# Attention and two feed-forward layers on one core: a planner that counts TensorE's turns between kinds of work

## Chip, core and metric

The kernel runs on one core of a Trainium2 chip. The metric is the device time of one execution in microseconds (us); lower is better.

## What is computed

Decayed causal attention (4 batches, 8 heads, 576 positions, head size 64), then two feed-forward layers over the 2304 tokens, all float32. Cut to what matters:

```python
scores = q @ k.T / sqrt(64) + cum[:, None] - cum[None, :]   # cum = cumsum(log f); causal
x = softmax(scores) @ v                       # heads side by side: (2304, 512)
h = x @ w_in                                  # (2304, 1024)
solu = h * softmax(h)
ln = (solu - mean) / sqrt(var + 1e-6) * g_ln
x2 = ln @ w_out                               # (2304, 512)
out = maximum(x2 @ w2_in, 0) ** 2 @ w2_out    # inner size 2048
```

## The kernel before

**Tiles.** Queries are cut into 20 tiles, five a batch: four of 128 rows and one of 64 (last in batches 0 and 2, first in 1 and 3). Tile n has eight heads; "n2h4" below is head 4 of tile 2.

**Steps on TensorE.** For each head `head` adds a step `scores` (L505: two matmuls, four where there are over 512 keys, float32r) and a step `flip` (L560: one transpose per block of keys, of the exponentials). For each pair of heads `mix` adds the product with the values (L581: plain float32, two TensorE records for each matmul), and after a tile's last pair `spread` (L608: four transposes). For each finished 128 tokens `first` adds the products with `w_in` (L808 to L810, 24 matmuls: "in" below), two steps of transposes (L885), and by way of `out1` the products with `w_out` (L749 to L751). `step` adds the second layer (up: L1146 to L1148, down: L1176 to L1178).

**Between them** VectorE takes a row minimum (L523, L526), ScalarE the exponential (L540) and most copies out of PSUM (L314). ScalarE, VectorE and GpSimd also turn Q, K and the weights into pairs of float32r (L316, L434, L661 to L679). `scores` writes PSUM banks z0 and z1; all transposes and `out1` share three banks (pp); the transposed exponentials go to a ring of three tiles (pt), so the copy for head s waits until the `mix` that read head s-3 is done.

**What sets the order.** No engine's order is written by hand. Each step is recorded by `Plan.add` with a duration on each engine, a due time `prio` and what it reads and writes; `Plan.lay` then places all of them, always the action that can start first. On each engine it takes the earliest start t0 of all candidates and, of those within `slack` (20 ns) of it, the one with the smallest `prio`:

```python
t0 = min(c[0] for c in cand)
c = min((c for c in cand if c[0] <= t0 + slack), key=lambda c: (c[1].prio, c[1].no))
```

For TensorE the end of a step follows from `pe_end`, which models a clock that halves after little work. Each engine then runs its instructions in that order. In the plan before, a step's duration depends on the step alone; `mix` carries a flat 200 ns.

Of the kernel before, what the change touches and what calls it, by code (L numbers as in the profile page):

```python
# [21 lines left out]


class Step:
    __slots__ = ("eng", "fn", "prio", "deps", "succ", "left", "rdy", "start", "end", "take", "uses", "on", "no", "late", "weak", "port")


class Plan:
# [10 lines left out]
        pe=dict(pe=0, dve=196, act=215, pool=200, dma=1100),  # L39
# [5 lines left out]

    TICK, DUTY = 10240 / 3, 1280.0

    def __init__(self, slots, banks):
        self.banks = banks
        self.steps = []  # L50
        self.writer = {}
        self.readers = {}
        self.slots = slots
        self.users = {}
        self.slot = {}

    def add(self, eng, fn, prio, reads=(), writes=(), take=None, uses=(), late=0, port=False):

        s = Step()
        s.eng, s.fn, s.prio, s.take, s.no, s.late = eng, fn, prio, take, len(self.steps), late
        deps = {}
        s.uses = tuple(uses) + ((take,) if take else ())
        for k in s.uses:
            self.users.setdefault(k, []).append(s)
        s.weak, s.port = None, port
        for k in reads:
            if k in self.writer:
                deps[self.writer[k].no] = self.writer[k]  # L70
            rs = self.readers.setdefault(k, [])
            if k in self.banks or k[0] == "pp":

                if rs and rs[-1].no not in deps:
                    s.weak = rs[-1]
                    deps[s.weak.no] = s.weak
            rs.append(s)
        for k in writes:
            if k in self.writer:
                deps[self.writer[k].no] = self.writer[k]  # L80
            for r in self.readers.get(k, ()):
                deps[r.no] = r
        for k in writes:
            self.writer[k] = s
            self.readers[k] = []
        deps.pop(s.no, None)
        s.deps = list(deps.values())
        s.succ = []
        for d in s.deps:
            d.succ.append(s)  # L90
        s.left = len(s.deps)
        s.rdy = {}
        s.end = None
        self.steps.append(s)
        return s

    def lay(self, slack=60):
# [48 lines left out]
                ready(s)  # L146
        todo = len(self.steps)
        port = 0.0
        order = []
        while todo:  # L150
            pick = None
            for e in engs:
                cand = []
                for s in avail[e]:
                    t = max(free[e], s.rdy[e])
# [15 lines left out]
                    cand.append((t, s, i))  # L171
                if not cand:
                    continue
                t0 = min(c[0] for c in cand)
                c = min((c for c in cand if c[0] <= t0 + slack), key=lambda c: (c[1].prio, c[1].no))
                if e != "pe":

                    end = c[0] + c[1].eng[e]
# [8 lines left out]
                if e == "pool":  # L187
# [5 lines left out]
                    ]  # L193
                    if any(y < end and end - y > (y - c[0]) * WORTH for y in x):
                        continue
                done = pe_end(c[0], c[1].eng[e], False) if e == "pe" else c[0] + c[1].eng[e]
                if pick is None or (c[0], done) < (pick[0], pick[4]):
                    pick = (c[0], c[1], c[2], e, done)
            assert pick, "the plan is stuck"
            t, s, i, e, done = pick  # L200
            if e == "pe":
                pe_end(t, s.eng[e], True)
            s.on, s.start, s.end = e, t, done
            free[e] = done
            if e == "dve" and s.port and s.eng[e]:
# [17 lines left out]
def tile_kernel(ctx: ExitStack, tc: tile.TileContext, q, k, v, f, w_in, w_out, g_ln, w2_in, w2_out, out):  # L223
# [257 lines left out]
    def head(s):  # L481
# [27 lines left out]
            rk += kcells(c, j, k0, k0 + ext)  # L509
        for c, k_ in zip(cuts, zk):  # L510
            mm = 0.4375 * rep * (c[2] - c[1]) + 6
            pl.add(dict(pe=2 * mm), lambda c=c: scores(c), prio, rk, [k_])
        st = ST[s % NST]
        su = SU[n % 2]
        adj = ADJ[s % NADJ]
# [37 lines left out]
        for g in range(0, nb, per):  # L553
            e = min(nb, g + per)
            sk = key()

            def flip(g=g, e=e, sk=sk):
                for c in range(g, e):
                    zc = zcol(T, c)
                    nc.tensor.transpose(at(sk)[:, (c - g) * m : (c - g + 1) * m], adj[0:m, zc : zc + P], ident[0:m, 0:m])  # L560

            pl.add(dict(pe=(e - g) * 109 * m / P), flip, prio - 200, ak + ["adjz"], [sk], take=sk)
            w = (e - g) * m
            copy(
                w, lambda g=g, e=e: pt[:, g * m : e * m], lambda sk=sk, w=w: at(sk)[:, 0:w], prio - 200, [sk],
                [("pt", s % NPT, g)], [sk],
            )


    def mix(s):  # L570
# [14 lines left out]
                    )  # L585

        rk = [("pt", (s - i) % NPT, g) for i in (0, 1) for g in range(5)] + [("vn", vslot[b, c]) for c in range(t + 1)]
        pl.add(dict(pe=(t + 1) * 218 * m / P + 200), fn, prio, rk, ["xo"])
        if p == NP - 1:
            i = T["x"] % XB  # L590
            w = slice(off, off + m)
# [32 lines left out]
                DM, lambda: X[0:m].rearrange("p c (j d) -> p (c j) d", d=D),  # L624
                lambda: su[0:m, 2].unsqueeze(2).broadcast_to([m, H, D]), prio - 300, [uk], ["x"], psum=False,
            )
            pl.add(dict(pe=NP * 109 * m / P), spread, prio - 300, ["x", "ident"], [sk], take=sk)
            copy(
                NP * m, lambda: X[:, :, 0:m], lambda: at(sk).rearrange("p (c x) -> p c x", x=P)[:, :, 0:m], prio - 300,
                [sk], ["x"], [sk],  # L630
# [162 lines left out]
    def first(x):  # L793
# [82 lines left out]
        for g in range(KF // 4):  # L876
# [15 lines left out]


            extra = [("lnr", y, z) for y in range(4) for z in "lh"] + [("lnw", y) for y in range(4)] if x == 0 else []
            pl.add(dict(pe=436), flips, t2 + g * 50, ["e", "ident"], [ck] + extra, take=ck)
            copy(
                512, lambda g=g: LN["h"][:, 4 * g : 4 * g + 4, x % 3, :],
                lambda ck=ck: at(ck).rearrange("p (c x) -> p c x", x=P), t2 + g * 50, [ck], [("lnh", x % 3, g)], [ck],
# [485 lines left out]

DUE, WORTH = 400, 1.0

_INS = ["q", "k", "v", "f", "moe_w_in", "moe_w_out", "moe_g_ln", "moe2_w_in", "moe2_w_out"]
_OUTS = [((2304, 512), "float32")]
# [43 lines left out]
```

## Time and profile before

| | |
|---|---|
| median of 3 runs | 875.02 us (873.55 to 877.12) |
| profiled execution | 874.1 us, its span 872.0 us |
| TensorE busy | 838.4 us (96%) |
| weight loads / VectorE / ScalarE / GpSimd busy | 83% / 52% / 56% / 33% |
| granted TensorE clock, mean | 0.987 |

The span runs from the first instruction to the last; the execution's time is 2.1 us more. A matmul's own duration overlaps that of the next one, so what a matmul costs TensorE is read from one start to the next.

### The profile page before, as it was taken

The page shows a single profiled execution, that of the slowest core. Times are in us where ns is not written, and L with a number is a line of the kernel's source. Part 1 is how long each engine was busy: PE and PEld are TensorE (multiplying, and loading weights), DVE is VectorE, ACT ScalarE, POOL GpSimd, SP SyncE. Part 2 cuts the span into 40 slices and gives each one's busy share as a digit, 9 for nine tenths or more (in the row PEclk, how much of TensorE's full clock was granted, in tenths as well). Part 3 has the DMA queues.
Part 4 walks back from the last instruction along what each step waited for, and adds up shares of the span by engine and source line. Part 5 has one row for each costly group of instructions (what it writes and reads, how often), then busy time and mean ns, then how long its engine had stood idle before and what let it go on. Part 6 is the DMA issues. An engine that isn't in the chain of part 4 may idle for free.

```text
span 872.0 us, 15164 instructions
## 1 busy us (share of the span) xinstructions
PE 838.4 (96%) x5360; PEld 727.3 (83%) x5360; DVE 449.1 (52%) x1152; ACT 485.1 (56%) x1237; POOL 283.5 (33%) x375
## 2 busy tenths in 40 slices
PE   4878999999999999999999999999999999999998
PEld 2556877888888887888898988989999999999997
DVE  7888776766766666865657475122222222222221
ACT  6899887777877667777656474224223223223222
POOL 7577765534643345433346474000000000000000
PEclk9998997999999999999999999999999999999999
DMA  6633343333542236332475630015003002000001
GB/s 210 197 96 104 112 138 112 122 103 99 168 140 86 86 92 181 109 105 89 137 224 175 194 116 6 1 35 183 1 1 109 0 2 97 13 1 12 26 0 37
DMA packets 61260, 81.04 MB, mean 93 GB/s; under 512 B 8096, under 2 KB 40352, under 8 KB 61184
## 3 DMA queue, kind: packets, MB, share of 16 engines
q1 hardware_dynamic: 61184, 80.07, 29.8%
q8 instruction: 42, 0.69, 0.3%
q14 instruction: 34, 0.28, 0.1%
HBM read 60.44 MB, written 19.55 MB: 92 GB/s over the span
## 4 chain that ended last, share of the span: by engine, by line
PE 85%; ACT 6%; DVE 4%; issue 2%; POOL 2%; DMA 1%; ACTq 0%; POOLq 0%; DVEq 0%
PE pp L1148 7%; PE pp L1147 7%; PE pp L1146 7%; PE pp L560 6%; PE xo L581 6%; PE z L505 6%; PE pp L749 4%; PE hp L808 4%; PE pp L750 3%; PE pp L751 3%; PE hp L810 3%; PE hp L809 3%; PE z L1176 2%; PE z L1178 2%; PE z L1177 2%
## 5 line engine op out<-in xcount | busy, mean ns | idle before, releaser
L1154 ACT ACTIVATE q<-pp 128x384 f32<-128x384 f32 x96 | 47.1, 490 | 242.4 <-PE pp L1148 240.0
L1157 DVE CAST q<-q 128x384 fp32r<-128x384 f32 x96 | 38.7, 403 | 267.5 <-PE xo L1178 92.3
L540 ACT ACTIVATE adj<-z,st 64x288 f32<-64x288 f32 (+9 forms) x192 | 95.0, 497 | 28.9 <-DVE st L526 27.6
L505 PE MATMUL z<-k,q 128*128 128x256 f32 (+17 forms) x384 | 96.4, 350 | 8.2 <-DVE q L470 8.2
L560 PE MATMUL pp<-ident,adj 128*128 128x128 f32 (+1 forms) x480 | 80.5, 284 | 15.5 <-ACT adj L540 14.6
L314 ACT COPY pt<-pp 128x256 f32<-128x256 f32 (+5 forms) x170 | 68.8, 422 | 35.6 <-PE pp L560 33.2
L560 PEld LDWEIGHTS pp<-ident,adj 128*128 128x128 f32 (+1 forms) x480 | 54.7, 146 | 36.3 <-ACT adj L540 24.3
L749 PE MATMUL pp<-ln,woh 128*128 128x256 f32 x288 | 83.4, 290 | 0.0
L526 DVE CUSTOM_DVE_ANT_0 z<-z,maskb 128x128 f32<-128x128 f32 (+8 forms) x144 | 65.8, 463 | 34.3 <-PE z L505 31.9
L750 PE MATMUL pp<-ln,wol 128*128 128x256 f32 x288 | 80.2, 279 | 0.0
L751 PE MATMUL pp<-ln,woh 128*128 128x256 f32 x288 | 80.2, 278 | 0.0
L505 PEld LDWEIGHTS z<-k,q 128*128 128x128 f32 (+3 forms) x384 | 59.8, 192 | 15.6 <-ACT pt L1267 8.2
L581 PE MATMUL xo<-pt,vn 128*64 128x128 f32 (+1 forms) x960 | 70.0, 279 | 0.2 <-ACT pt L314 0.2
L581 PEld LDWEIGHTS xo<-pt,vn 128*64 128x64 f32 x960 | 50.5, 141 | 19.9 <-issue 13.7
L808 PE MATMUL hp<-wih,xl 128*128 128x512 f32 x144 | 61.7, 428 | 1.8 <-ACT hp L847 1.0
L809 PE MATMUL hp<-wil,xh 128*128 128x512 f32 x144 | 57.6, 400 | 0.9 <-POOL wil L679 0.9
L810 PE MATMUL hp<-wih,xh 128*128 128x512 f32 x144 | 57.5, 399 | 0.0
L749 PEld LDWEIGHTS pp<-ln,woh 128*128 128x128 f32 x288 | 54.3, 188 | 2.7 <-issue 1.5
L750 PEld LDWEIGHTS pp<-ln,wol 128*128 128x128 f32 x288 | 54.3, 189 | 0.4
L751 PEld LDWEIGHTS pp<-ln,woh 128*128 128x128 f32 x288 | 54.2, 188 | 0.0
L1156 ACT ACTIVATE q<-q 128x384 f32<-128x384 f32 x96 | 50.4, 525 | 2.9
L540 ACT ACTIVATION_READ_ACCUMULATOR adj<-z,st 128x1 f32 (+1 forms) x192 | 37.8, 197 | 0.0
(503 smaller groups left out, 2180.2 us busy)
## 6 DMA issues: line engine op xcount, KB each, us to landing
x2d<-xc SPq DMA_DIRECT2D x72, 128.0 KB
kn<-in_k_dram SPq DMA_DIRECT2D x32, 256.0 KB
ws<-in_moe_w_out_dram SPq DMA_DIRECT2D x28, 256.0 KB
vn<-in_v_dram SPq DMA_DIRECT2D x20, 256.0 KB
ws<-in_moe_w_in_dram SPq DMA_DIRECT2D x20, 256.0 KB
ln<-x2d SPq DMA_DIRECT2D x24, 192.0 KB
out_dram<-pt SPq DMA_DIRECT2D x18, 256.0 KB
qn<-in_q_dram SPq DMA_DIRECT2D x16, 256.0 KB
```

Of the source, the lines that this page charges most:

```text
L314: nc.scalar.copy(dst(), src())
L505: nc.tensor.matmul(dst, lhsT=ql[0:r, p, 0:m], rhs=rhs, start=(g == 0), stop=(g == 1))
L526: nc.vector.tensor_tensor_reduce(out=z, in0=z, in1=maskb[0:m, o : o + e - a], scale=1.0, scalar=st[0:m, 0:1] if y else 3e38, op0=ALU.add, ...
L540: nc.scalar.activation(out=adj[0:m, c[1] : c[2]], in_=Z[c[0]][0:m, 0 : c[2] - c[1]], func=AF.Exp, bias=st[0:m, low : low + 1], scale=-1.0, ...
L560: nc.tensor.transpose(at(sk)[:, (c - g) * m : (c - g + 1) * m], adj[0:m, zc : zc + P], ident[0:m, 0:m])
L581: nc.tensor.matmul(XO[own[j], p, off : off + m], lhsT=VN[vslot[b, c]][:, (2 * p + j) * D : (2 * p + j + 1) * D], rhs=pts[j][:, c * m : (c ...
L749: nc.tensor.matmul(px, lhsT=woh[:, fc, w], rhs=lo, start=(fc == 0), stop=False)
L750: nc.tensor.matmul(px, lhsT=wol[:, fc, w], rhs=hi, start=False, stop=False)
L751: nc.tensor.matmul(px, lhsT=woh[:, fc, w], rhs=hi, start=False, stop=(fc == KF - 1))
L808: nc.tensor.matmul(HP[:, c], lhsT=XL[i][:, cc, :], rhs=wih[:, cc, w], start=(cc == 0), stop=False)
L809: nc.tensor.matmul(HP[:, c], lhsT=XH[i][:, cc, :], rhs=wil[:, cc, w], start=False, stop=False)
L810: nc.tensor.matmul(HP[:, c], lhsT=XH[i][:, cc, :], rhs=wih[:, cc, w], start=False, stop=(cc == KC - 1))
```

## The change

Each TensorE step gets a kind: `r` (all float32r matmuls of 128 rows), `h` (scores of a 64-row tile), `t` (transposes), `c` (the product with the values). A table gives a time in ns for each turn from one kind to another. In `lay`, on TensorE alone, a candidate's start is compared with its turn added, and among those within `slack` a candidate of another kind than the last step's is put 1000 ns later in due time. The turn is also added to the step's end. The flat 200 ns of `mix` goes. The other engines' rules stay.

```diff
+    TURN = dict(rt=20, tr=86, rc=93, tc=94, cr=250, ct=200, th=60, ht=100, rh=20, hr=10, hc=20, ch=200)
...
-                t0 = min(c[0] for c in cand)
-                c = min((c for c in cand if c[0] <= t0 + slack), key=lambda c: (c[1].prio, c[1].no))
+                if e == "pe":
+                    turn = {x[1]: self.TURN.get(kind + x[1].kind, 0) for x in cand}
+                    t0 = min(x[0] + turn[x[1]] for x in cand)
+                    near = [x for x in cand if x[0] + turn[x[1]] <= t0 + slack]
+                    c = min(near, key=lambda x: (x[1].prio + (HOLD if x[1].kind != kind else 0), x[1].no))
+                else:
+                    t0 = min(c[0] for c in cand)
+                    c = min((c for c in cand if c[0] <= t0 + slack), key=lambda c: (c[1].prio, c[1].no))
...
-                done = pe_end(c[0], c[1].eng[e], False) if e == "pe" else c[0] + c[1].eng[e]
+                done = c[0] + c[1].eng[e]
+                if e == "pe":
+                    done = pe_end(c[0], c[1].eng[e] + turn[c[1]], False)
...
             if e == "pe":
-                pe_end(t, s.eng[e], True)
+                pe_end(t, s.eng[e] + self.TURN.get(kind + s.kind, 0), True)
+                kind = s.kind
...
-            pl.add(dict(pe=2 * mm), lambda c=c: scores(c), prio, rk, [k_])
+            pl.add(dict(pe=2 * mm), lambda c=c: scores(c), prio, rk, [k_], kind="r" if m == P else "h")
...
-            pl.add(dict(pe=(e - g) * 109 * m / P), flip, prio - 200, ak + ["adjz"], [sk], take=sk)
+            pl.add(dict(pe=(e - g) * 109 * m / P), flip, prio - 200, ak + ["adjz"], [sk], take=sk, kind="t")
...
-        pl.add(dict(pe=(t + 1) * 218 * m / P + 200), fn, prio, rk, ["xo"])
+        pl.add(dict(pe=(t + 1) * 110 * m / P * 2), fn, prio, rk, ["xo"], kind="c")
...
+HOLD = 1000
```

`spread` and the transposes in `first` get kind `t` in the same way; everything else is `r`. No instruction is added or removed; the change is one of order, and of which engine takes a copy or a subtraction that more than one may take (VectorE 7 more, ScalarE 5 more, GpSimd 12 fewer of some 2,500).

**What moves, place 1.** TensorE, tile n8, heads 3 to 6 (line numbers of the changed file are higher by 15 from L505 on: L520 scores, L575 flip, L596 product with the values, L764 to L766 out1). Before:

```order
L560 MATMUL pp_122<-ident_68,adj_30_98 128x128 x4
L560 MATMUL pp_121<-ident_68,adj_31_99 128x128 x4
L505 MATMUL z_118<-k_9_77,q_13_81 128x448
L505 MATMUL z_118<-k_11_79,q_17_85 128x448
L581 MATMUL xo<-pt_32_100,vn_28_96 64x128
L581 MATMUL xo<-pt_33_101,vn_28_96 64x128
```

Now:

```order
L766 MATMUL pp_123<-ln_53_644,woh_74 128x256
L575 MATMUL pp_122<-ident_68,adj_29_97 128x128 x4
L575 MATMUL pp_121<-ident_68,adj_30_98 128x128 x4
L596 MATMUL xo<-pt_32_100,vn_28_96 64x128
L596 MATMUL xo<-pt_33_101,vn_28_96 64x128
```

Before, the flips of heads 3 and 4 (adj_30, adj_31) are followed by the scores of head 5 and then by the product for heads 2 and 3; now that product waits until the flips of heads 5 and 6 (adj_29, adj_30) and is entered from them.

**Place 2.** ScalarE, from the exponential of n2h2 to that of n2h4 (adj<-z is the exponential; q, wih, ln, xc, ws are conversions of Q and of weights; pt is a copy after a flip). Before:

```order
L540 ACTIVATE adj_29_97,su_39_107<-z_117,st_37_105 128x384
L316 ACTIVATE q_18_86<-qn_90 64x512
L314 COPY pt_34_102<-pp_121 128x384
L314 CAST wih_72<-ln_50_239 128x512
L314 COPY pt_32_100<-pp_122 128x384
L316 ACTIVATE q_14_82<-qn_90 64x512
L540 ACTIVATE adj_30_98,su_39_107<-z_118,st_38_106 128x384
L661 ACTIVATE xc_483<-xc_483 128x256
L316 ACTIVATE xc_483<-xc_483 128x256
L316 ACTIVATE q_19_87<-qn_90 64x512
L314 COPY pt_33_101<-pp_123 128x384
L661 ACTIVATE ws_497<-ws_497 128x256
```

(two rows further on, after one more cast of wih, stands the exponential of n2h4). Now:

```order
L555 ACTIVATE adj_29_97,su_39_107<-z_117,st_37_105 128x384
L676 ACTIVATE ln_50_240<-ln_50_240 128x512
L331 ACTIVATE ln_50_240<-ln_50_240 128x512
L329 COPY pt_32_100<-pp_122 128x384
L555 ACTIVATE adj_30_98,su_39_107<-z_118,st_38_106 128x384
L329 CAST wih_72<-ln_50_240 128x512
L329 COPY pt_33_101<-pp_123 128x384
L555 ACTIVATE adj_31_99,su_39_107<-z_117,st_35_103 128x384
```

Between the exponentials of n2h2 and n2h4 there are now six instructions where there were twelve: the conversions of Q and of xc and ws come later.

**Place 3.** TensorE, where the small 64-row tile n5 ends and n6 (192 keys) begins. Before, from the scores of n6h4 on:

```order
L505 MATMUL z_117<-k_9_77,q_13_81 128x192
L505 MATMUL z_117<-k_11_79,q_17_85 128x192
L581 MATMUL xo<-pt_32_100,vn_28_96 64x128
L581 MATMUL xo<-pt_33_101,vn_28_96 64x128
L581 MATMUL xo<-pt_32_100,vn_23_91 64x128
L581 MATMUL xo<-pt_33_101,vn_23_91 64x128
L885 MATMUL pp_121<-ident_68,e_116 128x128 x4
L560 MATMUL pp_122<-ident_68,adj_29_97 128x128 x2
```

Now:

```order
L900 MATMUL pp_121<-ident_68,e_116 128x128 x4
L596 MATMUL xo<-pt_32_100,vn_28_96 64x128
L596 MATMUL xo<-pt_33_101,vn_28_96 64x128
L596 MATMUL xo<-pt_32_100,vn_23_91 64x128
L596 MATMUL xo<-pt_33_101,vn_23_91 64x128
L823 MATMUL hp<-wih_72,xl_46_114 128x512
L824 MATMUL hp<-wil_73,xh_44_112 128x512
L825 MATMUL hp<-wih_72,xh_44_112 128x512
L575 MATMUL pp_123<-ident_68,adj_29_97 128x128 x2
```

The transposes L885 now stand ahead of the product with the values, and the first "in" matmuls of these 128 tokens follow it at once; before they came after the scores of n6h6.

## Rows read from the trace of the kernel before

**Rows 1.** Busy us by stretch: length, PE, PEld, DVE, ACT, POOL, clock, DMA, GB/s.

```profile
133.10:143.30 10.20, 9.47 (x45) 7.85 (x46) 5.71 (x20) 6.97 (x26) 6.08 (x9) 0.50 0.44 131
...
155.00:450.00 295.00, 294.27 (x2364) 252.65 (x2363) 200.12 (x587) 215.51 (x589) 126.95 (x175) 1.00 0.41 124
450.00:545.00 95.00, 92.88 (x518) 84.20 (x517) 58.28 (x117) 52.69 (x128) 53.32 (x66) 1.00 0.40 125
545.00:872.00 327.00, 323.37 (x1623) 292.41 (x1621) 70.75 (x154) 87.94 (x172) 0.00 (x0) 1.00 0.10 34
```

**Rows 2.** PE's waits from 8 to 66 us: us in total, times, longest.

```profile
PE pp L560 <- ACT adj L540: 10.3, 10, 2.8
```

**Rows 3.** ScalarE alone, an early stretch: length, busy us, clock, DMA, GB/s.

```profile
44.00:66.00 22.00, 20.64 (x50) 0.92 0.31 94
```

**Rows 4.** PE in order of time, turns to the product with the values: start us, length us.

```profile
186.78 1.09 PE L581 MATMUL xo<-pt,vn 128*64 128x128 f32 x16
187.81 0.65 PE L560 MATMUL pp<-ident,adj 128*128 128x128 f32 x4
...
199.94 0.40 PE L809 MATMUL hp<-wil,xh 128*128 128x512 f32 x1
200.18 0.39 PE L810 MATMUL hp<-wih,xh 128*128 128x512 f32 x1
200.50 1.31 PE L581 MATMUL xo<-pt,vn 128*64 128x128 f32 x20
201.74 0.50 PE L808 MATMUL hp<-wih,xl 128*128 128x512 f32 x1
202.08 0.39 PE L809 MATMUL hp<-wil,xh 128*128 128x512 f32 x1
```

**Rows 5.** PE in order of time, a turn to transposes and back; eight transposes elsewhere.

```profile
202.32 0.40 PE L810 MATMUL hp<-wih,xh 128*128 128x512 f32 x1
202.55 0.71 PE L560 MATMUL pp<-ident,adj 128*128 128x128 f32 x5
203.01 0.37 PE L749 MATMUL pp<-ln,woh 128*128 128x256 f32 x1
203.22 0.28 PE L750 MATMUL pp<-ln,wol 128*128 128x256 f32 x1
203.34 0.28 PE L751 MATMUL pp<-ln,woh 128*128 128x256 f32 x1
...
239.10 1.06 PE L885 MATMUL pp<-ident,e 128*128 128x128 f32 x8
239.92 0.48 PE L808 MATMUL hp<-wih,xl 128*128 128x512 f32 x1
```

**Rows 6.** ScalarE in order of time, the exponentials of n2h2, n2h4, n4h0, n7h0.

```profile
49.01 0.58 ACT L540 ACTIVATE adj<-z,st 128x384 f32<-128x384 f32 x1
...
55.40 0.57 ACT L540 ACTIVATE adj<-z,st 128x384 f32<-128x384 f32 x1
...
94.10 0.50 ACT L540 ACTIVATE adj<-z,st 64x288 f32<-64x288 f32 x1
...
146.22 0.53 ACT L540 ACTIVATE adj<-z,st 128x320 f32<-128x320 f32 x1
```

**Rows 7.** ScalarE's groups by form, 22 to 95 us: count, busy us, mean ns, idle before.

```profile
L661 ACT ACTIVATE ln<-ln 128x512 f32<-128x512 f32 x6 | 4.0, 673 | 0.0
L316 ACT ACTIVATE ln<-ln 128x512 uint32<-128x512 uint32 x6 | 4.0, 672 | 0.0
L314 ACT COPY pt<-pp 128x384 f32<-128x384 f32 x7 | 3.3, 473 | 0.0
...
L314 ACT CAST wih<-ln 128x512 fp32r<-128x512 f32 x4 | 2.4, 610 | 0.0
```

**Rows 8.** PE in order of time, start and end of the longest run of products and transposes.

```profile
302.77 0.60 PE L608 MATMUL pp<-ident,x 128*128 128x128 f32 x4
...
305.80 0.50 PE L808 MATMUL hp<-wih,xl 128*128 128x512 f32 x1
```

More of the change, by code (lines that the diff above doesn't have):

```diff
@@ L24 @@
 class Step:
-    __slots__ = ("eng", "fn", "prio", "deps", "succ", "left", "rdy", "start", "end", "take", "uses", "on", "no", "late", "weak", "port")
+    __slots__ = ("eng", "fn", "prio", "deps", "succ", "left", "rdy", "start", "end", "take", "uses", "on", "no", "late", "weak", "port", "kind")
 class Plan:
@@ L55, in __init__, with add @@
         self.slot = {}
-    def add(self, eng, fn, prio, reads=(), writes=(), take=None, uses=(), late=0, port=False):
+    def add(self, eng, fn, prio, reads=(), writes=(), take=None, uses=(), late=0, port=False, kind="r"):
         s = Step()
@@ L66, in add @@
             self.users.setdefault(k, []).append(s)
-        s.weak, s.port = None, port
+        s.weak, s.port, s.kind = None, port, kind
         for k in reads:
@@ L148, in lay @@
         port = 0.0
+        kind = "r"
         order = []
@@ L626, in mix @@
             )
-            pl.add(dict(pe=NP * 109 * m / P), spread, prio - 300, ["x", "ident"], [sk], take=sk)
+            pl.add(dict(pe=NP * 109 * m / P), spread, prio - 300, ["x", "ident"], [sk], take=sk, kind="t")
             copy(
@@ L894, in first @@
             extra = [("lnr", y, z) for y in range(4) for z in "lh"] + [("lnw", y) for y in range(4)] if x == 0 else []
-            pl.add(dict(pe=436), flips, t2 + g * 50, ["e", "ident"], [ck] + extra, take=ck)
+            pl.add(dict(pe=436), flips, t2 + g * 50, ["e", "ident"], [ck] + extra, take=ck, kind="t")
             copy(
```

## Prediction, written before the changed kernel had run

> **What bounds the kernel now.** I read the page, then the stretches, TensorE's waits, the order of time on TensorE and on ScalarE, and the groups by form. TensorE is busy 838.4 of 872.0 us (the page; in the table above). From 155 to 450 us, with attention and the first layer mixed, it is idle for 0.7 of 295 us; from 450 to 545 us for 2.1; after that it is full almost to the end [rows 1]. There, only less TensorE work makes the kernel shorter.
>
> The start is another matter. From 8 to 66 us flips wait 10.3 us for ScalarE's exponentials [rows 2], and from 44 to 66 us ScalarE is busy for 20.64 of 22 us [rows 3]: it is the bound there, and TensorE has too little other work. From 133.1 to 143.3 us TensorE is busy for 9.47 of 10.2 us, but its granted clock is 0.50, so 1.2 GHz instead of 2.4 [rows 1]; about half, 5.1 us, is lost. Before it TensorE did scores, transposes and products of the small 64-row tile n5, with hardly any of the dense first layer between.
>
> So three things can change the time: what turns cost on TensorE, which heads ScalarE serves early, and whether the slow stretch stays.
>
> **Turns on TensorE.** A visit to the product with the values costs time. Before one, the last matmul takes 0.32 us from its start to the next (200.18 to 200.50), where its like takes 0.24 (199.94 to 200.18): 0.08 more. Sixteen records, eight pairs, take 1.03 us, and 20 records take 1.24 [rows 4], about 0.11 a pair and 0.15 over. The first float32r matmul after takes 0.34 us (201.74 to 202.08) for 0.24: 0.10 more. In all about 0.33 us a visit.
>
> A visit to transposes costs nothing. The last matmul before them takes 0.23 us; five transposes take 0.46 and eight take 0.82, so each some 0.12; the first matmul after them takes 0.21 us (203.01 to 203.22) where the next takes 0.12 [rows 5]. What the first matmul loses, 0.09, the last transpose has already given, since the matmul starts early: 0.46 is 0.14 less than five times 0.12. Net at most 0.02 us.
>
> Now the count, from the printed order of both programs. Turns fall from 459 to 419 by the table's kinds. But those into the product are 80 in each, one for each pair of heads (from r, t and h: 54, 22 and 4 before, 9, 59 and 12 now). What falls is the turn from t to r, 119 to 75: 44 times at most 0.02 us, **0.0 to 0.9 us saved**. Leaving the product for r or h grows from 34 to 48 and for t falls from 46 to 32. The first transposes after a product cost about 0.05 us less than a matmul there (in the rows the 0.10 is for a matmul; for transposes I estimate half), so **up to 0.7 us lost**. I take nothing for the sum; bounds -0.9 and +0.7 us.
>
> The table itself prices t to r at 86 ns and leaves out what the last transpose gives back. By it the two orders would differ by 4.6 us (40.2 of turns before, 35.6 now). That is a rival below.
>
> **ScalarE's early order.** Place 2 shows the largest move. From the exponential of n2h2 to that of n2h4 ScalarE took 6.4 us [rows 6]. Of the new order the same piece comes to 0.57 + 0.67 + 0.67 + 0.47 + 0.57 + 0.61 + 0.47 = 4.0 us, by the forms in [rows 6, 7]. Pricing all its rows like that (each form's usual time to the next start), the work ahead of the exponential is less by 5.2 us at n2h4, 1.0 at n3h0, 4.4 at n3h4, 2.1 at n4h0; then more, by 1.9 us at n5h0 and 4.2 at n7h0. The work is put off and made up later. TensorE's own work ahead of the same heads is nearly unchanged (0.2 us more at n4h0, 0.1 less at n7h0), so where ScalarE is the bound the difference is TensorE's idle time. I take the value at n4h0, since from there on TensorE is kept full by the first layer: **-2.1 us**. The bounds are -4.4 (n3h4) and +0.9: VectorE, priced the same way, has 0.9 us more ahead of n3h4, and if it ends the waits the gain is a loss.
>
> From n4h0 to n7h0 ScalarE now has 6.3 us more to do, in a piece that took 52 us on the trace (94.1 to 146.2 [rows 6]) and held 40.7 us of ScalarE's work. That is 47 of 52, near the share of [rows 3], so flips may wait again. Bounds 0 and +3; I take **+0.5 us**, near the lower end, since TensorE has other work in most of this piece.
>
> **The slow stretch.** In place 3 transposes and a product now stand together, which is less of what keeps TensorE dense, and "in" matmuls come some heads earlier, which is more. If the clock stayed up, 5.1 us would be gained; if it stayed down twice as long, 5.1 lost. Nothing shows which, so I take 0 and both ends.
>
> Here a rule bears on the change. The longest run of products and transposes on the trace is from 302.77 to 305.80 us [rows 8], and the clock was 1.00 through all of 155 to 450 us [rows 1]. The new order has no longer run (by the rows' prices 2.8 us at most in both), but runs over 1.5 us hold 81 us of work in place of 38. The Trainium skill, "TensorE: Matmul & The Clock Gate", Part 4 (PE-mode transpose), says that transposes do not raise the clock as other matmuls do. By that rule grouping transposes with products would bring slow stretches in the middle, 5 us each; the 155 to 450 row speaks against it, the slow stretch after n5 for it. The sum goes by the row.
>
> **The middle and the seam.** The product for a pair now often comes after later flips (place 1), and so the pt tile that it reads is freed later, and the copy of head 5 there, which must wait for it, holds its pp bank longer; behind it on ScalarE stand the exponentials, and TensorE waits for those and for a pp bank for out1. Also, the plan now puts 86 ns on each of 75 turns from t to r which take none, so TensorE runs ahead of its plan, where before it ran behind (80 visits of 0.33 us planned at 0.2): other engines have less time in hand. If each of these turned into a wait, it would be 75 x 0.08 = 6 us; below, no more than today's 0.7 us idle can be gained. ScalarE is busy for 215 of 295 us and VectorE for 200 [rows 1], so I stay near the lower end, **+1 us**. From 450 to 545 us the 2.1 us idle may go or double: 0, bounds -2.1 and +2.1.
>
> GpSimd, with 12 operations fewer, and the DMA queue, with the same 452 entries in slightly another order, cost nothing as long as ScalarE or TensorE end the waits; their cover is the idle two thirds of GpSimd (busy 33% in the table).
>
> **Sum.** 0 - 2.1 + 0.5 + 0 + 1 + 0 = -0.6 us against the profiled execution's 874.1: 873.5. That execution is 0.9 us under the median of 875.0, so against the runs shown I give **874.4 us**.
>
> **Rivals.**
> *Early gain in full, and the clock stays up.* Heads come 4.4 us earlier and "in" matmuls fill the piece after n5: -4.4 - 5.1 + 1 + 0.5 = -8, so 875 - 8 = 867. For it: ScalarE does end the early waits. Against: VectorE has no less to do, and one missing dense stretch is enough for the clock.
> *The table is right.* If a turn from t to r did cost 0.086 us, 4.6 us go: 875.0 - 4.6 = 870.4. The rows speak plainly against it.
> *Slower by the clock.* In the middle a run of transposes and products after place 1's pattern lets the clock fall as at 133.1 us; one such fall of 10.2 us costs 5.1, so 875 + 5 = 880; it decides at the first row of clock 0.50 after 155 us.
> *Slower by waits.* TensorE ahead of its plan meets late copies, and the 6 us above become idle time before flips and out1: 880. It would need idle of some 80 ns at nearly every second flip between 155 and 450 us, where today there is almost none.
>
> **Chances.** A measurement of this kernel can tell about 0.5%, 4.4 us, from no change: faster is under 870.6, slower over 879.4. The forecast, with its own range of 870.6 to 878.5, has 0.47. The early gain with the clock has 0.24 and the table 0.05, so faster has 0.29. The clock in the middle has 0.11 and the waits 0.13, so slower has 0.24. The range should leave out at most 2 in 10: it reaches to the first rival's 867 and past the two slow ones' 880, **867 to 881**.
>
> **What would show it.** Right: the transposes' turns cost the same as before and TensorE's busy share from 155 to 450 us stays at 99%; the exponential of n2h4 starts some 3 to 5 us earlier than at 55.4 and that of n4h0 about 2 us earlier than 94.1 [rows 6]; flips wait less than 10.3 us from 8 to 66 us. Wrong: a second stretch of clock 0.50 after 110 us or none at all; waits on ScalarE's copies in the middle; a product whose visit costs clearly other than 0.33 us when entered from transposes; heads of tile n2 that come no earlier although ScalarE has less ahead of them, which would mean that VectorE or the loads set their pace.

## The result: slower by 1.3%

| | before | after |
|---|---|---|
| median of 4 runs each, side by side | 874.41 us (873.55 to 877.12) | 886.78 us (884.58 to 888.05) |
| profiled execution | 874.1 us, its span 872.0 us | 888.05 us, its span 886.2 us |

The ratio is 1.0133, with a 95% interval of 1.0118 to 1.0148: slower by more than the 0.5% that can be told from no change. The forecast was 874.4 us and the range ended at 881.

**The stretches after.** The kernel after, stretches; the columns are those of [rows 1]. Every line named here has a number higher by 15 in the kernel after (L314 is L329 there, L505 is L520).

```profile
44.00:66.00 22.00, 16.95 (x109) 11.84 (x109) 19.68 (x44) 19.61 (x48) 11.34 (x15) 0.89 0.31 91
66.00:110.00 44.00, 39.42 (x284) 31.99 (x283) 33.11 (x80) 39.08 (x99) 29.41 (x45) 0.95 0.34 104
110.00:155.00 45.00, 41.67 (x300) 32.97 (x301) 31.54 (x96) 35.67 (x116) 23.29 (x33) 0.85 0.46 141
155.00:450.00 295.00, 292.39 (x2345) 248.18 (x2344) 196.80 (x588) 211.49 (x582) 117.24 (x167) 1.00 0.37 111
450.00:545.00 95.00, 91.57 (x518) 81.40 (x517) 65.79 (x119) 55.86 (x136) 59.23 (x71) 1.00 0.51 159
```

And three of them in the kernel before:

```profile
44.00:66.00 22.00, 17.00 (x97) 11.70 (x98) 19.77 (x42) 20.64 (x50) 16.19 (x19) 0.92 0.31 94
66.00:110.00 44.00, 40.91 (x303) 33.75 (x302) 35.05 (x83) 40.35 (x102) 32.63 (x48) 0.92 0.36 113
110.00:155.00 45.00, 43.37 (x338) 34.18 (x337) 30.42 (x94) 34.15 (x112) 26.69 (x36) 0.89 0.40 122
```

From 66 to 155 us TensorE is busy for 3.2 us less after. From 155 to 450 it is idle for 2.6 us instead of 0.7, from 450 to 545 for 3.4 instead of 2.1 [rows 1]. From 44 to 110 us ScalarE did 2.3 us less, and from 110 to 155 us 1.5 more: part of the work put off came back there.

The flips' waits of [rows 2], from 8 to 66 us, have grown to 13.0 us. In the kernel after:

```profile
PE pp L575 <- ACT adj L555: 13.0, 10, 2.8
```

**Where the time went.** The same wall-clock stretch holds other work in the two kernels, so I cut both at the same steps. For each TensorE instruction I count its usual time to the next start (0.231 us for 512 columns in "in", 0.115 for out1's 256, 0.109 for a transpose of 128 rows, and so on, from both traces) and the price of each turn (the table of D4 below). This work is 809.6 us before and 809.5 after. What a piece takes beyond its work is called **lost** here: idle, slow clock and steps held up inside.

| lost us, profiled executions | before | after | more |
|---|---|---|---|
| to the first scores of n4 | 43.0 | 43.1 | 0.1 |
| n4 to n5 | 0.8 | 9.0 | 8.2 |
| n5 to n7 | 5.8 | 4.1 | -1.7 |
| n7 to the second layer | 4.9 | 10.1 | 5.2 |
| its first 200 up matmuls | 3.6 | 6.2 | 2.6 |

That is 14.4 us, against 14.0 between the two executions. Each number comes from the one profiled execution of its kernel.

**The wait after n4.** The kernel after, waits of TensorE from 66 to 155 us (us in total, times, longest), then TensorE and ScalarE in order of time there:

```profile
PE hp L823 <- ACT hp L862: 4.9, 1, 4.9
PE pp L575 <- ACT adj L555: 2.0, 1, 2.0
```

```profile
107.81 0.28 PE L766 MATMUL pp<-ln,woh 128*128 128x256 f32 x1
113.03 0.80 PE L823 MATMUL hp<-wih,xl 128*128 128x512 f32 x1 [4.94 <-ACT hp L862]
113.62 0.63 PE L824 MATMUL hp<-wil,xh 128*128 128x512 f32 x1
```

```profile
105.79 1.10 ACT L841 ACTIVATE e<-hp,sm 128x1024 f32<-128x1024 f32 x1
...
107.96 0.42 ACT L676 ACTIVATE ws<-ws 128x256 f32<-128x256 f32 x1
...
110.16 0.51 ACT L331 ACTIVATE ws<-ws,gcol 128x256 f32<-128x256 f32 x1 [0.80 <-POOL ws L690]
110.70 0.41 ACT L329 CAST woh<-ws 128x256 fp32r<-128x256 f32 x1
111.01 0.43 ACT L676 ACTIVATE xc<-xc 128x256 f32<-128x256 f32 x1
111.34 0.42 ACT L331 ACTIVATE xc<-xc 128x256 uint32<-128x256 uint32 x1
111.66 1.19 ACT L862 ACTIVATE hp<-e,sm 128x1024 f32<-128x1024 f32 x1
```

"In" for the next 128 tokens may overwrite hp only when the squares (L862, which ScalarE writes into hp) are through. Those stand behind conversions of ws and xc, one of which waits 0.80 us for GpSimd. Before, the exponential of h (the line with e<-hp) was at 101.03 and the squares at 104.81. The row maximum that this exponential needs ended at 96.38 us, 9.4 us ahead of it; before, the two lay 1.2 us apart. From n4h0 to this exponential ScalarE had hardly a gap (length, busy us, clock, DMA, GB/s):

```profile
95.35:105.79 10.44, 9.52 (x30) 1.00 0.49 149
```

TensorE's clock falls in this wait of 4.94 us: the kernel after has a stretch of 0.50 at 111.5 us, and the one of 133.1 us [rows 1] is now at 142.2.

**Why ScalarE was late: the scores of n3.** TensorE around the first scores of n3 (128x512), after, then before:

```profile
60.18 0.55 PE L575 MATMUL pp<-ident,adj 128*128 128x128 f32 x3
62.93 0.55 PE L575 MATMUL pp<-ident,adj 128*128 128x128 f32 x3 [2.20 <-ACT adj L555]
63.41 0.43 PE L596 MATMUL xo<-pt,vn 128*64 128x128 f32 x2
64.10 1.54 PE L596 MATMUL xo<-pt,vn 128*64 128x128 f32 x10 [0.26 <-ACT pt L329]
65.57 1.22 PE L520 MATMUL z<-k,q 128*128 128x512 f32 x2
```

```profile
61.10 0.55 PE L560 MATMUL pp<-ident,adj 128*128 128x128 f32 x3
61.40 0.72 PE L505 MATMUL z<-k,q 128*128 128x512 f32 x2
63.11 0.50 PE L808 MATMUL hp<-wih,xl 128*128 128x512 f32 x1 [0.99 <-ACT hp L847]
```

The exponentials they feed, in ScalarE's order of time after (n2h2, n2h4, n3h0, n4h0, n7h0):

```profile
49.45 0.57 ACT L555 ACTIVATE adj<-z,st 128x384 f32<-128x384 f32 x1
...
53.38 0.59 ACT L555 ACTIVATE adj<-z,st 128x384 f32<-128x384 f32 x1
...
67.68 0.69 ACT L555 ACTIVATE adj<-z,st 128x512 f32<-128x512 f32 x1 [1.26 <-DVE st L541]
...
95.35 0.50 ACT L555 ACTIVATE adj<-z,st 64x288 f32<-64x288 f32 x1
...
154.08 0.52 ACT L555 ACTIVATE adj<-z,st 128x320 f32<-128x320 f32 x1
```

From n2h2 to n2h4 ScalarE now takes 3.9 us instead of 6.4 [rows 6], as forecast. But after the flips of n2h6 the new choice keeps to its kind (to leave it is charged 86 ns): the flips of n2h7, whose exponential is not there (2.20 us of waiting), and the product stand ahead of the scores of n3h0. These come at 65.57 instead of 61.40, and ScalarE, 0.6 to 2.0 us ahead from n2h3 to n2h7, stands idle for 1.26 us until VectorE has read them. n4h0 is 1.25 us later than before [rows 6], not 2 us earlier. By then ScalarE has been busy for 77.93 us instead of 81.12 and idle for 4.4 us more; this place is the largest piece of that, the rest is spread over the time before it. The conversions are still owed. ScalarE's work from n4h0 to n7h0, before and then after (columns of [rows 1]):

```profile
94.10:146.20 52.10, 50.47 (x412) 41.28 (x412) 35.73 (x109) 42.02 (x136) 33.42 (x46) 0.90 0.44 134
```

```profile
95.35:154.08 58.73, 52.88 (x416) 43.24 (x410) 42.09 (x122) 47.75 (x149) 33.45 (x47) 0.88 0.46 141
```

The runs below bear this out as far as plans can: with the old rule or this table, the six in which the scores of n3h0 start at 65.3 us or later (after, E1, E2, S3, S4, G1) lose 6.4 us or more from n4 to n5, and the nine in which they start at 58.9 to 62.6 us lose 0.8 to 4.9. No run moves these scores alone.

### The profile page after: what moved, and what is told of

It reads as the page before. It is cut to its first block, busy times and chain, and to the rows that moved or that the text cites. A ratio compares the mean times of both kernels' runs of the same rounds, so it can differ in the third digit from the quotient of the medians.

```text
span 886.2 us, 15207 instructions
## 1 busy us (share of the span) xinstructions
PE 845.6 (95%) x5360; PEld 729.7 (82%) x5360; DVE 455.4 (51%) x1159; ACT 486.0 (55%) x1242; POOL 267.8 (30%) x363
## 4 chain that ended last, share of the span: by engine, by line
PE 78%; ACT 6%; DVE 5%; issue 2%; POOL 1%; DMA 1%; SPq 0%; ACTq 0%; POOLq 0%; DVEq 0%
PE pp L1163 7%; PE pp L1162 7%; PE pp L1161 7%; PE z L520 6%; PE xo L596 5%; PE pp L575 5%; PE hp L823 4%; PE pp L764 3%; PE pp L765 3%; PE pp L766 3%; PE hp L825 3%; PE hp L824 3%; PE hp L1191 2%; PE z L1191 2%; PE hp L1192 2%; PE z L1193 2%
## 5 line engine op out<-in xcount | busy, mean ns | idle before, releaser
L520 PE MATMUL z<-k,q 80*64 80x288 f32 (+17 forms) x384 | 97.3, 351 | 8.3 <-DVE q L485 8.2
L575 PE MATMUL pp<-ident,adj 128*128 128x128 f32 (+1 forms) x480 | 79.0, 279 | 16.6 <-ACT adj L555 15.7
L329 ACT COPY pt<-pp 128x256 f32<-128x256 f32 (+5 forms) x170 | 68.5, 422 | 37.2 <-PE pp L575 28.6
L575 PEld LDWEIGHTS pp<-ident,adj 128*128 128x128 f32 (+1 forms) x480 | 52.0, 142 | 40.3 <-ACT adj L555 29.9
L764 PE MATMUL pp<-ln,woh 128*128 128x256 f32 x288 | 82.2, 285 | 1.0 <-DVE ln L903 1.0
L541 DVE CUSTOM_DVE_ANT_0 z<-z,maskb 128x128 f32<-128x128 f32 (+8 forms) x144 | 65.3, 464 | 33.6 <-PE z L520 28.3
L766 PE MATMUL pp<-ln,woh 128*128 128x256 f32 x288 | 80.6, 280 | 0.0
L520 PEld LDWEIGHTS z<-k,q 128*128 128x128 f32 (+3 forms) x384 | 58.7, 189 | 19.9 <-ACT pt L1282 8.2
L596 PE MATMUL xo<-pt,vn 128*64 128x128 f32 (+1 forms) x960 | 70.2, 278 | 0.7 <-ACT pt L329 0.6
L596 PEld LDWEIGHTS xo<-pt,vn 128*64 128x64 f32 x960 | 50.6, 140 | 16.7 <-issue 11.8
L764 PEld LDWEIGHTS pp<-ln,woh 128*128 128x128 f32 x288 | 54.7, 190 | 3.6 <-DVE ln L903 1.6
L766 PEld LDWEIGHTS pp<-ln,woh 128*128 128x128 f32 x288 | 54.7, 190 | 0.0
```

Of the source, the lines that this page charges most:

```text
L329: nc.scalar.copy(dst(), src())
L520: nc.tensor.matmul(dst, lhsT=ql[0:r, p, 0:m], rhs=rhs, start=(g == 0), stop=(g == 1))
L541: nc.vector.tensor_tensor_reduce(out=z, in0=z, in1=maskb[0:m, o : o + e - a], scale=1.0, scalar=st[0:m, 0:1] if y else 3e38, op0=ALU.add, ...
L596: nc.tensor.matmul(XO[own[j], p, off : off + m], lhsT=VN[vslot[b, c]][:, (2 * p + j) * D : (2 * p + j + 1) * D], rhs=pts[j][:, c * m : (c ...
L764: nc.tensor.matmul(px, lhsT=woh[:, fc, w], rhs=lo, start=(fc == 0), stop=False)
L766: nc.tensor.matmul(px, lhsT=woh[:, fc, w], rhs=hi, start=False, stop=(fc == KF - 1))
```

## Experiments

Times are medians beside runs of the kernel before in the same batch (874.6 to 875.3 us in each). The letters in the expectations: **W**, the one wait for the squares costs most; **T**, the new order's turns cost more everywhere; **S**, scatter: any new plan differs by some us; **R**, the new rule itself; **P**, the planned pace of TensorE against its real one; **C**, the choice by kind.

### First batch: one wait, and halves of the rule

E1, steps from exponential to squares of the third 128 tokens set right behind what they need, in the printed order:

```diff
...
+    for x in (2,):
+        for s in CH[x]:
+            s.start = max(d.end + pl.LAT[d.on][s.on] for d in s.deps)
+            s.end = s.start + s.eng[s.on]
+    order.sort(key=lambda s: (s.start, s.no))
```

> The changed kernel with one thing moved: for the third block of 128 tokens (x = 2) the exponential of h, the four small VectorE steps behind it and the square that frees the bank pair hp are put as early in their queues as what they read allows; TensorE's order is untouched. Theory W (the loss is waits that the new order makes, above all the one of 4.9 us at 108 us where the first matmul of the next block waits for that square, and the half clock after it): 6 to 8 us come back, 879 to 881. Theory T (turns and late products cost TensorE time everywhere): at most 1 us comes back, 886.

Measured: 890.06 us (1.0174, 1.0155 to 1.0194). E1's waits of TensorE from 66 to 155 us:

```profile
PE z L520 <- ACT adj L555: 4.4, 2, 3.5
PE pp L575 <- ACT adj L555: 4.2, 3, 2.0
```

The wait for the squares is gone and the heads' exponentials are late instead (n4h1 at 103.07 us, behind the moved steps, instead of 100.81): lost from n4 to n5 13.6 us. W fails as put: more than this one step is late there.

E2, the new rule only until 125 us of the plan, then the old one; E3 the reverse:

```diff
+                on = free["pe"] < CUT
+                turn = {}
+                if e == "pe" and on:
...
+CUT = 125000
```

> The new rule and its times until the plan's clock reads 125 us, the old rule (and 200 ns a product) after it. Theory W: the wait near 108 us is there, the later waits are not, so 7 to 10 us slower than before, 881 to 884. Theory T: one seventh of the loss, 876. Theory S (any new plan scatters, whatever the rule): the early part is the same as in the changed kernel, so it also gives 881 to 884, but the rest may differ by 2 us either way.

> The old rule until the plan's clock reads 125 us, the new rule after it. Theory W: the early wait is gone; the waits from 155 to 545 us stay, 4 to 6 us slower than before, 878 to 880. Theory T: nearly the whole loss, 884 to 886.

E4, the new choice with the old planned times:

```diff
-                    done = pe_end(c[0], c[1].eng[e] + turn[c[1]], False)
+                    done = pe_end(c[0], c[1].eng[e], False)
...
+        pl.add(dict(pe=(t + 1) * 218 * m / P + 200), fn, prio, rk, ["xo"], kind="c")
```

> The new choice between candidates with the old times: turns are compared and kinds preferred, but no turn is added to a step's end and the product keeps its 200 ns. Theory T: as slow as the changed kernel, 885 to 888, since TensorE's order has the same grouping. Theory W: what decides is where the waits fall, and with other times the early wait falls elsewhere or not at all: 874 to 883. If it is as fast as before, the added times are what makes the loss.

Measured: E2 881.73 us (1.0066 to 1.0096), E3 883.90 (1.0091 to 1.0123), E4 879.98 (1.0045 to 1.0075). E2 has the early loss and the old middle, E3 the late one: two separate losses. (E3's early part is that of S1 below: it too plans the product at 220 ns a matmul.) T falls: TensorE's work with its turns is the same, and E4, which groups the kinds as much (408 turns), loses least. Most of E4's 5.4 us lie ahead of n4, in neither of the two places.

### Second batch: how much is scatter

S1: the kernel before with `220` for `218` in `mix`. S2: the kernel before with `SLACK = 25` for 20. S3: the kernel after with `218` for `220`. S4: the kernel after with `HOLD = 0`.

> The kernel before, with its old rule, whose product with the values is planned at 220 ns for each matmul instead of 218. Theory S (scatter: the plan before is a lucky one, and any new plan loses a few us early or in the middle): 877 to 884 us. Theory R (the new rule itself is what costs): within 2 us of the kernel before, 872.5 to 876.5.

> The kernel before, with its old rule, whose slack for comparing starts is 25 ns instead of 20. Theory S: 877 to 884 us, idle time before n5 or between n7 and the second layer larger by 2 us or more. Theory R: within 2 us of the kernel before.

> The changed kernel, whose product is planned at 218 ns a matmul instead of 220. Theory S: anywhere from 877 to 890 us, and the 8 us between n4 and n5 change by 3 us or more. Theory R: within 2 us of the changed kernel's 886.8, the wait for the squares at 113 us still there.

> The changed kernel with the 1000 ns of due time for another kind taken away (turns are still counted in starts and ends). Theory R, with the choice as the cost: 875 to 879 us, middle idle 5 us instead of 10. Theory R, with the planned times as the cost: 883 to 888. Theory S: anywhere from 877 to 890, no relation to either part.

Measured: S1 879.73 us (1.0031 to 1.0061), S2 **872.45** (0.9963 to 0.9984), S3 883.50 (1.0077 to 1.0114), S4 887.51 (1.0100 to 1.0158). Neither theory holds as put: S1 is what S expects, S4 fits R (and S, which allows almost anything there), S2 and S3 fit neither. Two ns in a planned duration cost the kernel before 4.4 us; but no near copy of the kernel after comes below 882. Taking `HOLD` away changes nothing that can be told. That fits the table: most of its turns are longer than the slack of 20 ns, so a later due time seldom has anything left to decide between kinds. S2 beats the kernel before, by 0.3%.

### Third batch: the planned pace

D1 and D2: the kernel before with `+ 0` and `+ 450` for `+ 200` in `mix` (a visit really takes about 330). D3: the table in the planned ends with the old choice. D4: the table replaced by the prices from the traces, with 64-row transposes as a kind `u` of their own:

```diff
+    TURN = dict(rt=4, tr=4, ru=144, ur=198, hu=142, uh=145, tu=144, ut=149, uc=139, cu=150, rc=143, cr=208, tc=144, ct=157, hc=142, ch=145, hr=3)
```

> The kernel before, whose product carries no flat time at all instead of 200 ns a visit (measured: about 330), so that TensorE runs some 26 us behind its plan over 80 visits. What is read is the idle time from n7 to the second layer, 5.0 us before and 10.1 after. Theory P (the plan's TensorE being slower than the chip's costs waits in the middle): 3 to 5 us idle there. Theory S (any new plan scatters): anything from 4 to 10. The total follows the early part: 870 to 882.

> The kernel before, with its old rule, whose product carries 450 ns a visit (measured: about 330), so that TensorE runs some 10 us ahead of its plan. Theory P: 8 to 12 us idle from n7 to the second layer, as after, although the rule of choice is the old one and the turns into transposes are as many as before. Theory S: no relation, 4 to 10. Theory C (the choice by turns is what costs): 5.

> The changed kernel's times (the table counted in each step's end, no flat 200 ns) with the old choice (earliest start, then due time). Theory P: 8 to 11 us idle from n7 to the second layer. Theory C: 5 us there. Total 878 to 889.

> The changed kernel with the table replaced by the turns that the traces show: r to t and t to r 4 ns, into the product 143, out of it 208 to r and 157 to t, transposes of 64 rows some 145 each way. TensorE then keeps its plan's pace. Theory P: 5 to 8 us idle from n7 to the second layer, between before and after. Theory S: anything from 4 to 10. Theory C: 10, since the choice stays.

Measured: D1 881.31 us (1.0049 to 1.0090), D2 880.51 (1.0042 to 1.0078), D3 882.04 (1.0047 to 1.0099), D4 901.53 (1.0281 to 1.0322). What the first expectations call "idle from n7 to the second layer" is the lost time of that piece. For all plans of this kind, with G1 and G3 from further down (lost us; D3's profiled execution is 2.9 us under its median, the others 2 us or less from theirs):

| run | choice | planned pace | to n4 | n4 to n5 | n5 to n7 | n7 to second layer | TensorE idle 155 to 440 us |
|---|---|---|---|---|---|---|---|
| before | old | visit 200 ns | 43.0 | 0.8 | 5.8 | 4.9 | 0.7 |
| S1 | old | visit 200 | 43.5 | 4.6 | 5.7 | 4.7 | 0.6 |
| S2 | old, slack 25 | visit 200 | 41.3 | 2.0 | 1.7 | 7.5 | 3.1 |
| D1 | old | visit 0 | 45.2 | 4.9 | 4.6 | 4.2 | 0.7 |
| E4 | new | visit 200 | 46.5 | 2.5 | 5.8 | 5.1 | 1.1 |
| G3 | new, slack 25 | visit 200 | 45.4 | 0.8 | 5.1 | 4.7 | 0.6 |
| E2 | new early | visit 200 late | 44.1 | 9.1 | 3.8 | 5.1 | 0.7 |
| D2 | old | visit 450 | 46.9 | 1.0 | 1.1 | 9.9 | 3.3 |
| D3 | old | table | 45.8 | 1.7 | 0.9 | 11.1 | 3.0 |
| E3 | new late | table late | 43.9 | 4.8 | 5.4 | 8.1 | 1.8 |
| after | new | table | 43.1 | 9.0 | 4.1 | 10.1 | 2.6 |
| S3 | new | table | 42.9 | 6.4 | 1.2 | 9.8 | 2.1 |
| S4 | new | table | 43.8 | 9.0 | 4.3 | 10.6 | 1.8 |
| G1 | new, slack 25 | table | 43.9 | 8.9 | 4.7 | 12.2 | 3.3 |

The idle column is 285 us less TensorE's busy time, as in these rows for E4, D3 and D2:

```profile
155.00:440.00 285.00, 283.89 (x2304) 245.12 (x2305) 191.72 (x574) 206.00 (x575) 122.97 (x175) 1.00 0.38 115
```

```profile
155.00:440.00 285.00, 282.03 (x2258) 237.65 (x2257) 192.90 (x565) 207.41 (x578) 108.55 (x159) 1.00 0.37 111
```

```profile
155.00:440.00 285.00, 281.73 (x2272) 238.92 (x2271) 191.09 (x563) 205.38 (x570) 118.09 (x167) 1.00 0.37 112
```

The middle, n7 to the second layer, goes with the planned pace, whatever the choice: 4.2 to 5.1 us lost where TensorE is planned faster than it is (S2's 7.5 apart), 8.1 to 12.2 where it is planned at the table or slower. D2 shows it with one number of the kernel before. By the same count of work and turns, TensorE needs in this piece 10 us more than planned in the kernel before, 22 more in D1, and 2.6 to 6.8 us less in the kernel after, D2 and D3. Not all of this reaches the total: D2, D3 and S3 lose 4.6 to 4.9 us less than the kernel before from n5 to n7, where they have no slow stretch, so from n5 to the second layer D2 loses 11.0 us against 10.7. Over that longer piece the two groups just part: 8.8 to 10.9 us (S2 among them) and 11.0 to 16.9.

The early loss needs both halves of this change: 6.4 us or more with choice and table together, 4.9 or less with one or none. That holds for this table alone; F1, F2, F3 and G2 below, with other tables for the choice and the old planned times, lose 9.0 to 12.1 us there.

### Fourth and fifth batch: what the choice does with true prices

D4 lost 28.4 us in the middle, against P's 5 to 8, although by the same count TensorE is within 1.3 us of its plan there: P does not explain it. F1: D4's table for the choice alone, old planned times. F2: as F1 with the eight entries of `u` alone. F3: F2 with a slack of 25. G2: F2 with `HOLD = 0`. G1: the kernel after with a slack of 25. G3: E4 with a slack of 25.

> The measured table used for the choice alone; each step's planned time is the old one (product with its flat 200 ns), so that TensorE runs behind its plan as before. TensorE's own work is less by 9.3 us than before (384 turns, 68 visits to the product, 21 to transposes of 64 rows). If the planned times made the 28 us of waits with the measured table: 5 to 8 us idle from n7 to the second layer and 865 to 875 in all. If the choice made them (products put one behind the other before their copies are there): 15 us or more idle there and 882 to 895.

> The choice knows only the turns of transposes of 64 rows (each some 145 ns), all others are free; planned times are the old ones. TensorE's own work is less by 4.7 us than before. If the loss of the changed kernel lies in planned times and in scatter, not in choosing by kind as such: 5 us idle in the middle, 868 to 876 with the scatter of the early part. If any choice by kind costs: 877 or more.

> As the run of the small turns alone, with a slack of 25 ns. TensorE's own work is 4.5 us less than before. If the early part is scatter, it differs from the run with 20 ns by 3 us or more early or after n4, in either direction: 865 to 880. If a slack of 25 ns as such is what helped the kernel before: 866 to 870, no slow clock after 100 us.

> The changed kernel with a slack of 25 ns instead of 20, which made the kernel before 2 to 3 us faster. If choosing and planning by the table costs in itself: lost time from n4 to n5 of 6 us or more (0.8 before, 8.1 after) and 8 to 11 us from n7 to the second layer, 880 to 890 in all, as in the changed kernel's other near copies. If scatter alone made the loss: as likely 872 to 880, with less than 4 us lost from n4 to n5.

> The choice by the turns of 64-row transposes alone, with the 1000 ns of due time for another kind taken away. If that due time used up the matmuls of in and out1 ahead of n15 (138.3 us of them where 125.9 stood before): some 126 us ahead of n15, no slow clock at 362 us, 872 to 880. If the counted turns of the small transposes did: 138 us again, and 895 to 910.

> The new choice with the old planned times and a slack of 25 ns. If the gain of 25 ns belongs to the slack: 872 to 878, 3 to 8 us under the same kernel with 20 ns (880.0). If it was scatter: 876 to 884, and the piece from n4 to n5 anywhere from 1 to 5 us.

Measured: F1 901.01 us (1.0276 to 1.0315), F2 904.59 (1.0320 to 1.0357), F3 910.35 (1.0388 to 1.0426), G1 889.37 (1.0137 to 1.0181), G2 902.10 (1.0297 to 1.0327), G3 876.05 (1.0002 to 1.0021). F2's stretches, then those of the kernel before at the same tiles:

```profile
340.00:355.00 15.00, 14.80 (x126) 14.16 (x125) 9.80 (x27) 8.23 (x21) 7.78 (x10) 1.00 0.51 151
355.00:362.40 7.40, 5.92 (x73) 4.11 (x73) 3.26 (x11) 4.57 (x17) 1.16 (x3) 1.00 0.20 68
362.40:386.30 23.90, 22.29 (x134) 16.91 (x133) 11.12 (x47) 15.78 (x61) 9.51 (x13) 0.50 0.44 127
```

```profile
333.00:337.90 4.90, 4.90 (x49) 3.53 (x47) 3.42 (x13) 3.86 (x16) 3.48 (x6) 1.00 0.57 176
337.90:354.00 16.10, 16.10 (x140) 13.74 (x139) 12.23 (x48) 14.10 (x51) 9.21 (x12) 1.00 0.59 174
```

In F1, F2, F3, G2 and D4 alike, 576 out1 and 312 in matmuls stand ahead of the first scores of the small tile n15; before, 480 and 306. The first layer has by then no more to give, and in F2 from 355 us on TensorE has heads alone and waits for their exponentials and copies. Its clock falls to 0.50 for 23.9 us in F2, 6.8 to 23.9 in the five, where the kernel before, with out1 between the heads, is full at 1.00. The choice made it (F1 has the old times), and in it the counted turns, not the due time (G2). The rule says how: while TensorE is on kind `r`, every matmul of that kind that could start now beats a 64-row transpose that is due, since 144 ns are more than the slack. In F2 no flip runs from 326 to 353 us, while in and out1 do. G1 confirms the early loss with the table (8.9 us from n4 to n5, 12.2 in the middle). G3, with the new choice at the old pace, is within 0.2% of the kernel before: choosing by the table of the change need not cost. A slack of 25 ns gained 2.9 us in S2 and 3.9 in G3 and lost 2.6 in G1 and 5.8 in F3; so it scatters, and S2 is a good plan rather than a better rule.

## Why the prediction was wrong

**ScalarE's early order (-2.1 taken): the step that failed first.** The rows were priced rightly (4.0 us forecast from n2h2 to n2h4, 3.9 measured), but n2h2 itself came 0.4 us later, so n2h4 was 2.0 us earlier and not 3 to 5, and the flips waited 13.0 us where less than 10.3 was forecast. The claim that the difference is TensorE's idle time held within n2 alone: from the scores of n2h0 to those of n2h4 TensorE lost 3.0 us instead of 6.8, but 2.2 more ahead of n2h0, and from n2h4 to the scores of n3h0 7.4 instead of 3.1; 2.7 us of this came back by n4h0. I priced ScalarE's order and not what feeds it: the scores of n3h0 had been put behind flips that wait for ScalarE. Measured at n4: 0.1 us lost instead of 2.1 gained.

**n4h0 to n7h0 (+0.5 taken, 0 to +3): the largest miss.** Measured +6.5 us (8.2 - 1.7). The count of ScalarE's work was right (6.3 us more forecast, 5.7 measured: 47.75 instead of 42.02). The step that failed is the cover, that TensorE has other work meanwhile: it had, but "in", the very work meant as cover, waited 4.94 us for ScalarE itself. The share of 47 of 52 us hid this, since ScalarE is full ahead of the wait (9.52 of 10.44 us) and has time left behind it. E1 points the same way: with that wait taken away, other waits for ScalarE's steps take its place. That the 6.5 us are ScalarE's 5.7 us of late work, one for one, is not shown.

**The slow stretch (0, ±5.1).** Stretches of 0.50 from n4 to n7 are 13.6 us long instead of 10.2, so 1.7 us of those 6.5 are the clock. Inside the bounds, but not by place 3: the new stretch at 111.5 us falls into the wait of 4.94 us, and the old one has moved to 142.2 us with the tiles and is shorter (6.8 instead of 10.2 us).

**The middle (+1 taken, -0.7 to +6).** Measured +5.2. The mechanism named, TensorE no longer behind its plan, is the one that D1, D2, D3 and E4 bear out for this piece; the size was off, since I took ScalarE's mean share for time in hand. How far ahead was off too, since it left out that a visit to 64-row transposes costs some 0.34 us: counted with it, TensorE is ahead of the new plan by only 2.6 us in this piece, where it was behind the old one by 10. Of the 5.2 us, 1.9 are visible as idle; the rest lies in steps that took longer than usual without an idle gap in the profile, and what held them up stays open.

**The seam (0, ±2.1).** +2.6 here; over the other plans it goes from 3.2 to 10.3 us lost, with no relation to the rule that I could find. The bound was today's idle time, and the measured loss is past it.

**Turns (0): right.** The work is the same within 0.1 us, with 40 turns fewer. Two readings behind it were off without harm: a transpose takes 0.109 us and not 0.12, and visits to 64-row transposes were counted as free, but there are 32 before and 31 after. Entered from transposes, sixteen records of the product take 1.02 us (1.03 in [rows 4]):

```profile
202.48 0.71 PE L575 MATMUL pp<-ident,adj 128*128 128x128 f32 x5
203.12 1.09 PE L596 MATMUL xo<-pt,vn 128*64 128x128 f32 x16
204.14 0.54 PE L520 MATMUL z<-k,q 128*128 128x288 f32 x2
```

**The rivals.** The table as a gain fell with that. The clock in the middle did not fall (1.00 from 155 to 450 us after), though more of the work lies in long runs of transposes and products. The Trainium skill, "TensorE: Matmul & The Clock Gate", Part 4 (PE-mode transpose), says that transposes do not raise the clock as other matmuls do. For the middle the row was the better guide. In F2 the clock falls in a piece of heads alone, but TensorE is idle for 1.48 of the 7.4 us ahead of it. Ahead of the fall at 142.2 us in the kernel after it is hardly idle at all, with little but heads of n5 and n6:

```profile
138.00:142.20 4.20, 4.11 (x29) 2.94 (x27) 3.06 (x16) 3.74 (x17) 1.80 (x5) 1.00 0.42 138
```

So the clock can fall without a wait. Whether transposes do it, or the other small steps of these heads, no run here tells. "Slower by waits" had the sign and, in the middle, nearly the size (5.2 us against 6), though most of it not as visible idle time; its place was wrong, since the greater part lies from n4 to n5, and flips were not the only ones to wait.

**The range.** Its upper end lay just past the rivals that let one thing go wrong at a time. The upper bounds of the pieces add up to 17.8 us, and the 14.0 measured lie inside that: here the early piece, the middle and the seam went wrong together. It also left out that any new plan moves the early part: the old rule's five plans (before, S1, S2, D1, D2) lose 0.8 to 4.9 us from n4 to n5, and the kernel before is the best of them there. How the 12.4 us of loss divide is not shown. Alone, the choice costs 5.4 us (E4), the table in the planned times 7.3 (D3) and a change of 2 ns 4.4 (S1), and they lose it in other pieces than the kernel after does.

## What to carry to other kernels

A greedy scheduler that charges an engine for changing its kind of work looks after that engine and can starve those that it feeds: here the charge put scores behind flips that waited, and with true prices it used up the filler work ahead of the tile that needed it. Where one engine is the bound, try planning it somewhat faster than it runs, so that the others have time in hand; here that went with a middle of 4 to 5 us lost (7.5 in S2) instead of 8 to 12, though D1, planned fastest, lost 6.5 us in all by other pieces. Count a turn's price against what the next step feeds. And before a difference of 0.5% between two plans is put down to a rule, change something that means nothing (2 ns) and see how far the time moves.

## Not expected of the hardware

A turn between 128-row transposes and float32r matmuls costs TensorE nothing that can be measured (some 4 ns each way over both traces), while a visit to transposes of 64 rows costs about 0.34 us (144 ns in, 198 out to float32r matmuls, fitted over both traces), as much as one to the plain float32 product (143 in, 208 out). Ahead of such a transpose the last matmul of 512 columns takes 0.327 us to the next start, where its like takes 0.231. D4, planned by these, has 9.8 us less TensorE work by the same count, 799.8 us; it was lost many times over in waits, and a plan that keeps both was not found in these runs.
